# First attention of a fused attention and two-MoE kernel: memory products in two banks, one reciprocal per sequence, loads per sequence, and a new written order

## The chip, the cores and the metric

One core of a Trainium2 chip runs the kernel. The metric is the time of one execution on the device in microseconds (us), as the median over runs. The engines are named as the profile names them: PE is TensorE (matmuls), PEld its weight loads, DVE is VectorE, ACT is ScalarE, POOL is GpSimd and SP is SyncE, which issues all the DMA transfers.

## The reference, cut to what matters

Four sequences of 576 tokens with 8 heads of 64 go through an attention that adds a memory readout, and then through two gated layers with 512 to 1536 to 512 columns. All inputs are f32.

```python
scores = scale * (q @ k.T);  scores[causal] = -1e9          # per batch b, head h
a = exp(scores - scores.max(-1));  a /= a.sum(-1) + 1e-9
local = a @ v
q_p = where(q > 0, q, exp(q) - 1) + 1                       # phi
mem_out = (q_p @ M_prev) / ((q_p @ z_prev) + 1e-6)
g = sigmoid(beta)                                           # per head
x = g * mem_out + (1 - g) * local                           # -> tokens x 512
x = x / sqrt(mean(x * x) + 1e-6) * rms_g
x = (silu(x @ w_gate) * (x @ w_val)) @ w_out                # first MoE layer
x = (sigmoid(x @ w_gate2) * (x @ w_val2)) @ w_out2          # second MoE layer
```

## The kernel before, in words

The tokens go through the layers in five groups. Group -1 holds the first 128 tokens of each of the four sequences (512 tokens); groups 0 to 3 hold the other 448 tokens of one sequence each. While the layers of group g run on TensorE, the attention of group g + 1 is issued in between. A layer works in 12 slices of 128 hidden columns. For each slice `hidden` makes two products, `pg` (gate) and `pv` (value), VectorE and ScalarE make the gated product `t` from them, and `out_share` adds its product with the slice's output weights to the four accumulators `po`. The weights arrive as 64-bit floats (`raw`, `rawl`), ScalarE and VectorE take each block to f32 (`f64_top`, `f64_word`), and split it into a high and a low part.

The change is in what stands ahead of all that: the first attention, that of group -1, which nothing can hide (`att_first`). Its stages are small functions, made for each sequence b and often for each half j of the heads (j = 0 even, j = 1 odd heads), and the string `ORDER` names them in the order in which they are written. A stage's instructions are tied to the one before it on the same engine, so `ORDER` is the order of each engine's queue up to its last name:

- `S` scores of a sequence into two banks, `M` maxima, `X` exponentials, `T` transposes, `C` copies of the transposed weights, `A` products with v;
- `E`, `Em`, `Ph` the feature function phi (ScalarE, GpSimd, VectorE), `P` memory products, `R` and `V` the divisions of memory and local part, `Y` their sum on GpSimd;
- `Q`, `N`, `W`, `F` square, mean, power and norm, `U` transposes of the normed tokens, `H` and `L` their high and low part;
- `wt`, `wo`, `wh`, `wl` the four weight blocks (gate and value) of slices 0 and 1: top, word, high, low;
- `g0a`, `v0a`, `a0a`, `dd0a` (and `g1a` ...) gate, value, tanh and gated product of slices 0 and 1 for the first 256 tokens, the two first sequences;
- `fillN` N matmuls whose result nobody reads, and `G`, `G1` the gates from beta.

Behind `ORDER`, a scheduler places what `hidden`, `weights` and `token_scale` issue, as far as `issue_after` leaves it open. It starts with the second 256 tokens of slices 0 and 1, whose products `pg` and `pv` go into the two banks of the pool `mm`. `out_share` of slice 0 follows, and then slice 2. Weight loads go through four buffers `raw` and two `rawl`; the tile `warm`, which the fillers read, lies in one of the four. `token_scale` takes the largest entry of the norm's weights `g_bc` (`gm`) and scales them for the later groups. SP issues DMAs in the order of its queue, and a `kept` transfer that waits for a word holds those behind it.

Of the kernel before, what the change touches and what calls it, by code (L numbers as in the profile page):

```python
# [9 lines left out]
F32 = mybir.dt.float32  # L10
# [50 lines left out]
def attn_moe_moe_kernel(ctx, tc, qT, kT, qk0, v, mz, beta, w8, rms_g, outT):  # L61
# [6 lines left out]
    nc = tc.nc  # L68
# [36 lines left out]
    ones = const.tile([128, 1], F32, name="ones")  # L105
# [3 lines left out]
    bt = const.tile([128, H], F32, name="bt")  # L109
# [13 lines left out]
    pw = zps.tile([128, 512], F32, tag="fb", name="pw")  # L123
# [94 lines left out]

    def att_load0():
        for b in range(B):  # L220
            z["e", b] = zp.tile([128, NMAX], F32, tag=f"ze{b % 2}", name="e0")
            qk = zp.tile([128, 2, NMAX], F32, tag=f"zqk{b}", name="qk0")
            z["q", b], z["k", b] = qk[:, 0], qk[:, 1]
            nc.sync.dma_start(out=qk, in_=qk0[b])
            if b == 0:
                first_raw.append(load_raw(0, 0, 0))
            if b == 1:
                nc.sync.dma_start(out=bt, in_=beta[None, :].to_broadcast([128, H]))
                z["v"] = zp.tile([128, B, NMAX], F32, tag="zv", name="v0")
                nc.sync.dma_start(out=z["v"], in_=v[:, 0:128, :].rearrange("b s d -> s b d"))  # L230
                load_consts()
            if b == 2:
                first_raw.append(load_raw(0, 0, 1))
        for m in range(2):
            first_raw.append(load_raw(0, 1, m))

    def first_stages(xt):
# [43 lines left out]
        def exps(b, j):  # L281
            z["rs", b, j] = ap_.tile([128, NP], F32, tag="rs", bufs=8, name="rs")
            sc = z["sc", b, j] = zp.tile([128, NMAX], F32, tag=f"zs{j}", bufs=2, name="s0")
            for p in range(NP):
# [7 lines left out]
                    accum_out=z["rs", b, j][:, p:p + 1],  # L292
# [27 lines left out]
        def av_mul(b, j):  # L320
# [1035 lines left out]
```

## Time and profile before

| | before |
|---|---|
| median of 3 runs | 1050.18 us (1047.84 to 1050.64) |
| profiled execution | 1048.04 us |
| span of the profiled execution, first to last instruction | 1046.3 us |
| mean granted TensorE clock | 0.998 of 2.4 GHz |
| PE busy | 1024.9 us (98% of the span) |
| DVE busy | 815.1 us (78%) |
| ACT busy | 590.6 us (56%) |
| POOL busy | 90.8 us (9%) |

The profiled execution lasts 1.7 us longer than its span. Busy shares are means over the whole span; the first 60 us look different from the rest, and have to be read by themselves.

### The profile page before, as it was taken

The page shows a single profiled execution, that of the slowest core. Times are in us where ns is not written, and L with a number is a line of the kernel's source. Part 1 is how long each engine was busy: PE and PEld are TensorE (multiplying, and loading weights), DVE is VectorE, ACT ScalarE, POOL GpSimd, SP SyncE. Part 2 cuts the span into 40 slices and gives each one's busy share as a digit, 9 for nine tenths or more (in the row PEclk, how much of TensorE's full clock was granted, in tenths as well). Part 3 has the DMA queues.
Part 4 walks back from the last instruction along what each step waited for, and adds up shares of the span by engine and source line. Part 5 has one row for each costly group of instructions (what it writes and reads, how often), then busy time and mean ns, then how long its engine had stood idle before and what let it go on. Part 6 is the DMA issues. An engine that isn't in the chain of part 4 may idle for free.

```text
span 1046.3 us, 18459 instructions
## 1 busy us (share of the span) xinstructions
PE 1024.9 (98%) x6801; PEld 774.2 (74%) x6801; DVE 815.1 (78%) x1751; ACT 590.6 (56%) x1118; POOL 90.8 (9%) x85
## 2 busy tenths in 40 slices
PE   8899999999999999999999999999999999999998
PEld 5768887888766777776667867666677777987896
DVE  5969999988759989874677866648788768995882
ACT  5758877776768868862454543425545444542442
POOL 3301001000002102110010101000101000000000
PEclk9999999999999999999999999999999999999999
DMA  7499998984898457678554553585556257846630
GB/s 272 161 360 364 317 389 258 312 275 168 239 348 276 147 213 240 246 249 279 199 168 163 173 187 130 152 281 168 167 174 211 90 175 231 309 146 221 238 121 36
DMA packets 92281, 231.63 MB, mean 221 GB/s; under 512 B 24096, under 2 KB 30240, under 8 KB 92064
## 3 DMA queue, kind: packets, MB, share of 16 engines
q1 hardware_dynamic: 92192, 230.47, 65.2%
q8 instruction: 53, 0.87, 0.3%
q14 instruction: 36, 0.29, 0.1%
HBM read 182.72 MB, written 44.04 MB: 217 GB/s over the span
## 4 chain that ended last, share of the span: by engine, by line
PE 78%; DVE 9%; issue 5%; DMA 4%; ACT 3%; SPq 0%; POOL 0%; ACTq 0%; DVEq 0%; POOLq 0%
PE po L863 23%; PE pg L807 20%; PE pv L807 19%; PE pw L973 6%; PE ps L210 4%; PE pm L580 1%; PE pav L531 1%; PE pav L533 1%; PE pav L532 1%; DMA g_bc<-in_rms_g 1%; DMA ha<-x 1%; PE po L860 1%; DMA raw<-in_w 1%; DMA half<-ws 0%; DVE x L624 0%
## 5 line engine op out<-in xcount | busy, mean ns | idle before, releaser
L863 PE MATMUL po<-h,ws 128*128 128x448 f32 (+1 forms) x468 | 114.3, 385 | 0.2 <-DMA ws<-parts 0.2
L863 PE MATMUL po<-h,wl 128*128 128x448 f32 (+1 forms) x408 | 99.6, 385 | 0.0
L863 PEld LDWEIGHTS po<-h,ws 128*128 128x128 f32 x468 | 86.0, 188 | 11.9 <-ACT h L846 0.4
L515 POOL PARTITION_ALL_REDUCE mb<-mx x32 | 57.0, 1783 | 406.6 <-DVE mx L511 394.7
L827 ACT ACTIVATE t<-pg,unit 128x448 f32<-128x448 f32 x70 | 44.2, 631 | 73.7 <-PE pg L807 73.7
L863 PE MATMUL po<-h,wr 128*128 128x448 f32 x360 | 85.6, 379 | 0.0
L863 PEld LDWEIGHTS po<-h,wl 128*128 128x128 f32 x408 | 75.5, 188 | 9.7 <-ACT h L842 0.2
L807 PEld LDWEIGHTS <-ws 128*128 128x128 f16 x504 | 46.8, 98 | 46.8 <-issue 6.2
L807 PEld LDWEIGHTS <-wr 128*128 128x128 f16 x504 | 46.8, 98 | 44.3 <-issue 4.4
L475 ACT COPY sc<-ps 128x448 f32<-128x448 f32 (+5 forms) x128 | 51.9, 421 | 41.7 <-DVE sc L470 20.8
L842 ACT CAST h<-t 128x448 fp32r<-128x448 f32 (+1 forms) x70 | 40.6, 580 | 55.4 <-DVE t L831 50.5
L863 PEld LDWEIGHTS po<-h,wr 128*128 128x128 f32 x360 | 66.7, 188 | 6.1
L201 ACT ACTIVATE sc<-sc 128x1536 f32<-128x1536 f32 x32 | 47.5, 1485 | 38.1 <-DVE sc L524 26.6
L204 DVE TENSOR_TENSOR pt<-sc,pt 128x1536 f16<-128x1536 f32 x32 | 56.1, 1754 | 10.0 <-ACT pt L203 9.7
L807 PEld LDWEIGHTS <-wl 128*128 128x128 f16 x384 | 35.9, 98 | 33.9 <-issue 4.2
L210 PE MATMUL ps<-qq,kk 128*128 128x448 f32 (+2 forms) x160 | 57.9, 365 | 1.0 <-ACT sc L475 1.0
L843 DVE TENSOR_TENSOR h<-t,h 128x448 fp32r<-128x448 f32 (+1 forms) x70 | 46.2, 659 | 10.8 <-ACT h L842 10.5
L829 DVE SCALAR_TENSOR_TENSOR t<-t,pg 128x448 f32<-128x448 f32 (+2 forms) x50 | 31.0, 620 | 26.3 <-ACT t L827 26.3
L210 PE MATMUL ps<-q,kk 128*128 128x448 f32 (+2 forms) x160 | 49.4, 318 | 0.0
L837 DVE SCALAR_TENSOR_TENSOR t<-t,pv 128x448 f32<-128x448 f32 (+1 forms) x52 | 32.9, 632 | 20.5 <-PE pv L807 19.1
L203 ACT CAST pt<-sc 128x1536 f16<-128x1536 f32 x32 | 47.0, 1468 | 0.3
L807 PEld LDWEIGHTS <-wrl 128*128 128x128 f16 x288 | 26.6, 98 | 26.5 <-issue 3.8
(330 smaller groups left out, 2672.2 us busy)
## 6 DMA issues: line engine op xcount, KB each, us to landing
raw<-in_w SPq DMA_DIRECT2D x50, 511.8 KB, 6.5
ws<-parts SPq DMA_DIRECT2D x32, 512.0 KB, 4.1
wr<-parts SPq DMA_DIRECT2D x32, 512.0 KB, 3.9
wl<-parts SPq DMA_DIRECT2D x26, 512.0 KB, 3.7
kept<-w SPq DMA_DIRECT2D x48, 256.0 KB, 5.3
rawl<-in_w SPq DMA_DIRECT2D x22, 511.8 KB, 7.0
ws<-half SPq DMA_DIRECT2D x21, 512.0 KB, 3.7
wr<-half SPq DMA_DIRECT2D x19, 512.0 KB, 4.1
```

Source lines behind the costliest of these rows:

```text
L201: nc.scalar.activation(out=sc[:, 0:n], in_=sc[:, 0:n], func=AF.Exp, scale=scale)
L203: nc.scalar.copy(out=pt[:, 0, 0:n], in_=sc[:, 0:n])
L204: nc.vector.tensor_tensor(out=pt[:, 1, 0:n], in0=sc[:, 0:n], in1=pt[:, 0, 0:n], op=ALU.subtract)
L210: nc.tensor.matmul(ps[:, c0:c0 + n], kk[:, k0:k0 + 128], r[:, q0:q0 + n], start=(i == 0), stop=(i == 1 and not mask))
L475: nc.scalar.copy(out=sc[:, d:d + n], in_=ps[:, c:c + n])
L515: nc.gpsimd.partition_all_reduce(mb[:, 0:448], mx[:, 0:448], channels=128, reduce_op=bass_isa.ReduceOp.max)
L807: nc.tensor.matmul(ps[:, 0:n], w[:, a, k * 128:(k + 1) * 128], x[b][:, k, o:o + n], start=(i == 0), stop=(i == 3 * KD - 1))
L827: nc.scalar.activation(out=t, in_=pg[:, 0:n], func=AF.Tanh, scale=u[:, 0:1] if half else 0.5)
L842: nc.scalar.copy(out=hi, in_=t)
L843: nc.vector.tensor_tensor(out=lo, in0=t, in1=hi.bitcast(F32), op=ALU.subtract)
L863: nc.tensor.matmul(po[d][:, 0:n], w[2][:, a, c], hh[:, b, 0:n], start=(first and i == 0), stop=(last and i == 2))
L973: nc.tensor.matmul(regions[m][at], left(i, m, a, k), right(j, b, k), start=first and c == 0, stop=c == 5, skip_group_check=True,)
```

## The change

The stages of the first attention are rewritten and reordered.

- Memory products: one stage `P` per sequence fills two banks with the products of all 8 heads, in place of two stages with one bank each.
- Division: `D` makes all 16 divisors of a sequence with one reciprocal (8 for the local part, 8 for the memory part), and `Vm` and `Va` do one 512-wide multiply each. Before there were four groups of combination, reciprocal and 256-wide multiply. Both halves' products with v now go into one bank.
- Loads: `v` and the memory matrices come per sequence, in an order of their own (`LOADS`); beta comes as one row and is spread over the partitions by a one-row matmul (`G0`).
- The copies of the transposed weights all go to ScalarE; before, two of them went to VectorE.
- There are 18 fillers in place of 36, and they read the identity in place of `warm`.
- Slice 1's second 256 tokens get two banks of the pool `ps`. `token_scale` stands behind the last stage of `ORDER`, `dd1a`. The weights of slices 2 to 4 are written behind the gated product of slice 1.

```diff
 ORDER = """
-E0 S0 Em0 wt0 Ma0 Mb0 S1 fill3 Xa0 wo0 Ph0 fill1 Xb0 Ta0 fill1 Ma1 Mb1 Ca0 Tb0 fill1 Xa1 Aa0 fill1
...
+S0 S1 fill4 G0 E0 Ma0 wt0 E1 Em0 Xa0 fill2 Ta0 Mb0 Em1 G1 Ph0 Xb0 P0 Ca0 wo0 E2 fill2 Tb0 Cb0 Ma1
+Mb1 G Xa1 Aa0 fill1 Ab0 wt1 S2 D0 Vm0 Va0 Xb1 Em2 Ph1 wo1 Ta1 Mb2 Y0 Q0 N0 P1 Tb1 Ca1 D1 E3 Xb2
...
-COPY = "DDAA"
...
+    banks = [zps.tile([128, 512], F32, tag=f"pp{i}{j}", name="pw") for i in (0, 2, 1) for j in range(2)]
+    pw = banks[3]
...
+    LOADS = "q0 q1 w0 v0 m0 b q2 v1 m1 g w1 v2 m2 q3 v3 m3 w2 w3"
...
+        def gates_sum():
+            z["bt"] = zps.tile([128, H], F32, tag="pm", name="pb")
+            nc.tensor.matmul(z["bt"], ones, bt, start=True, stop=True)
...
         def fill(n):
             for i in range(n):
-                nc.tensor.matmul(pw, warm[:, 0:128], warm, start=True, stop=True)
+                nc.tensor.matmul(
+                    z.get("unread", pw).rearrange("p (a k) -> p a k", a=4),
+                    ident_b,
+                    ident_b[:, None, :].to_broadcast([128, 4, 128]),
+                    start=True,
+                    stop=True,
+                )
...
-            if j == 0 or COPY[b] == "A":
-                nc.scalar.copy(out=pt, in_=z["ps", b][j])
-            else:
-                nc.vector.tensor_copy(pt, z["ps", b][j])
+            nc.scalar.copy(out=pt, in_=z["ps", b][j])
+            if j:
+                z["unread"] = z["ps", b][1]
...
+        def divisors(b):
+
+            r = z["r", b] = ap_.tile([128, 2, H], F32, tag="r1", bufs=2, name="r1")
+            sums = z["pm"][:, :, 0:260].rearrange("p i (h d) -> p i h d", d=65)[:, :, :, 64]
             nc.vector.scalar_tensor_tensor(
...
+                out=r[:, 0], in0=z["rs", b], scalar=1e-9, in1=igate1, op0=ALU.add, op1=ALU.mult
+            )
...
             nc.vector.reciprocal(out=r, in_=r)
+
+        def mem_mul(b):
             nc.vector.tensor_tensor(
...
+                out=x[:, b, :].rearrange("p (i h d) -> p i h d", i=2, d=64),
+                in0=z["pm"][:, :, 0:260].rearrange("p i (h d) -> p i h d", d=65)[:, :, :, 0:64],
+                in1=z["r", b][:, 1].rearrange("p (i h) -> p i h", i=2)[:, :, :, None].to_broadcast([128, 2, 4, 64]),
                 op=ALU.mult,
             )
...
             for f in range(early):
-                hidden(ws[f], l, f, 256, g, xt, hs[f], 256)
+                hidden(ws[f], l, f, 256, g, xt, hs[f], 256, (("mm", "mm"), ("ps", "pa"))[f])
+                halfway.append(tuple(last_of(e) for e in (mybir.EngineType.Activation, mybir.EngineType.DVE)))
...
-                        with behind(turn):
+                        with behind(turn + (halfway[-1:] if early and f < early + 3 else [])):
                             ws.append(weights(g, l, f))
...
             if l == 0 and g < 0:
-                token_scale()
+                with tc.issue_after(z["gm"]):
+                    token_scale()
```

VectorE, around the first division. Before, its queue holds these rows between the maxima of sequence 1 (`m` from `ps_192`) and the first local division of sequence 0:

```order
L278 TENSOR_REDUCE m_231<-ps_192 128x4
L674 TENSOR_REDUCE gm<-g_bc 128x1
L279 TENSOR_SCALAR m_231<-m_231 128x4
L306 COPY qk_131<-ps_172 128x512
L657 TENSOR_SCALAR pw<-gm 128x1
L659 TENSOR_SCALAR inv<-pw 128x1
L246 TENSOR_SCALAR igate<-igate 128x8
L246 TENSOR_SCALAR igate_100<-igate_100 128x8
L663 RECIPROCAL s_2226<-inv 128x1
L676 TENSOR_SCALAR half_isx<-inv 128x1
L325 SCALAR_TENSOR_TENSOR r_263<-rs,igate_100 128x4
L333 RECIPROCAL r_263<-r_263 128x4
```

With the change the same place, from the same maxima (`ps_197`) on, holds the whole division of sequence 0:

```order
L291 TENSOR_REDUCE m_265<-ps_197 128x4
L292 TENSOR_SCALAR m_265<-m_265 128x4
L249 TENSOR_SCALAR igate<-igate 128x8
L249 TENSOR_SCALAR igate_100<-igate_100 128x8
L337 SCALAR_TENSOR_TENSOR r_298<-rs,igate_100 128x8
L340 SCALAR_TENSOR_TENSOR r_298<-pm,igate 128x8
L348 RECIPROCAL r_298<-r_298 128x16
L351 TENSOR_TENSOR x<-pm,r_298 128x512
L360 TENSOR_TENSOR av<-ps_184,r_298 128x512
```

The `gm` chain (`gm`, `pw`, `inv`, `s`, `half_isx`) and the copy from `ps_172` have left this place, and one reciprocal serves both divisions.

VectorE, at the end of the first attention. Before, from the low part of sequence 2's tokens (`xb` from `ps0_305`) on (numbers tell buffers apart), with the output weights' words (`wo`) and slice 2's first words between the gated products `t`:

```order
L400 TENSOR_TENSOR xb_156<-ps0_305,xa_155 128x4x128
L386 SCALAR_TENSOR_TENSOR qk0_149<-x_159,ri_161,g_bc_101 128x512
L456 SCALAR_TENSOR_TENSOR t_157<-t_157,pg_560 128x256
L677 TENSOR_SCALAR g_bc_101<-g_bc_101,s2_2226 128x512
L457 TENSOR_TENSOR t_157<-t_157,pv_577 128x256
L737 SCALAR_TENSOR_TENSOR wo_650<-raw_651,top0_126 128x512
L737 SCALAR_TENSOR_TENSOR wo_657<-raw_658,top1_128 128x512
L400 TENSOR_TENSOR xb_156<-ps0_415,xa_155 128x4x128
L737 SCALAR_TENSOR_TENSOR w_730<-raw_731,top0_126 128x512
L456 SCALAR_TENSOR_TENSOR t_158<-t_158,pg_600 128x256
L737 SCALAR_TENSOR_TENSOR w_740<-raw_741,top1_128 128x512
L457 TENSOR_TENSOR t_158<-t_158,pv_615 128x256
```

With the change, from the last gated product of the first 256 tokens on:

```order
L486 TENSOR_TENSOR t_172<-t_172,gv_532 128x256
L703 TENSOR_REDUCE gm_2169<-g_bc_101 128x1
L686 TENSOR_SCALAR pw_2171<-gm_2169 128x1
L688 TENSOR_SCALAR inv_2173<-pw_2171 128x1
L692 RECIPROCAL s2_2175<-inv_2173 128x1
L705 TENSOR_SCALAR half_isx_126<-inv_2173 128x1
L706 TENSOR_SCALAR g_bc_101<-g_bc_101,s2_2175 128x512
L858 SCALAR_TENSOR_TENSOR t_171<-t_171,pg_613 128x256
L864 TENSOR_TENSOR t_171<-t_171,pv_626 128x256
L858 SCALAR_TENSOR_TENSOR t_172<-t_172,pg_642 128x256
L864 TENSOR_TENSOR t_172<-t_172,pv_655 128x256
L766 SCALAR_TENSOR_TENSOR w_679<-raw_680,top0_131 128x512
```

All four gated products of the second 256 tokens (`L858`, `L864`) now stand ahead of the first word of slice 2 (`w`), and the `gm` chain stands ahead of them.

SP, where the loads of slices 0 to 3 follow the four first ones. Before (`kept` writes a finished word back, `raw` and `rawl` load a block):

```order
L751 DMA kept_0_0_213<-w_162 128x512
L751 DMA kept_0_0_213<-w_164 128x512
L725 DMA raw_651<-in_w8 128x2047
L751 DMA kept_0_1_430<-w_166 128x512
L725 DMA raw_658<-in_w8 128x2047
L751 DMA kept_0_1_430<-w_168 128x512
L725 DMA raw_731<-in_w8 128x2047
L725 DMA raw_741<-in_w8 128x2047
L725 DMA rawl_750<-in_w8 128x2047
```

With the change:

```order
L780 DMA kept_0_0_252<-w_176 128x512
L754 DMA raw_600<-in_w8 128x2047
L780 DMA kept_0_0_252<-w_178 128x512
L754 DMA raw_607<-in_w8 128x2047
L780 DMA kept_0_1_478<-w_180 128x512
L754 DMA raw_680<-in_w8 128x2047
L780 DMA kept_0_1_478<-w_182 128x512
L754 DMA raw_690<-in_w8 128x2047
L754 DMA rawl_699<-in_w8 128x2047
L754 DMA rawl_761<-in_w8 128x2047
```

Slice 2's first two blocks are the last two `raw` in both. Now each of them stands behind a `kept` of slice 1 (`kept_0_1`), so behind that block's word; the two `rawl` follow as before.

## Rows read from the trace of the kernel before

**Rows 1.** The chain that ended last: start us, us, what.
```profile
20.72 0.44 PE ps L298 x4
...
60.58 3.43 PE po L860 x8
```

**Rows 2.** Waits by engine and line: us in total, times, longest us.
```profile
DVE gm L674 <- DMA g_bc<-in_rms_g: 3.1, 1, 3.1
...
PE ps L312 <- DVE pw L657: 2.9, 1, 2.9
...
PE pg L807 <- DVE t L829: 1.7, 1, 1.7
...
SPq L725 <- PE pw L272: 3.9, 1, 3.9
```

**Rows 3.** Windows: stretch, its length, busy us by engine, PEclk, DMA share, GB/s.
```profile
15.00:20.00 5.00, 3.58 (x18) 3.23 (x19) 4.00 (x19) 2.02 (x9) 0.67 (x1) 0.71 1.03 413
...
60.00:80.00 20.00, 20.00 (x77) 13.94 (x77) 11.53 (x20) 9.93 (x16) 0.00 (x0) 1.00 1.03 370
80.00:160.00 80.00, 80.00 (x467) 65.26 (x466) 78.68 (x148) 64.92 (x107) 7.77 (x4) 1.00 1.00 352
```

**Rows 4.** Timeline of VectorE: start us, us, line, operation, out<-in.
```profile
8.41 0.68 DVE L278 TENSOR_REDUCE m<-ps 128x4 f32<-128x512 f32 x1
...
9.22 0.69 DVE L737 SCALAR_TENSOR_TENSOR w<-raw,top 128x512 int32<-128x512 int32 x1
9.83 0.69 DVE L354 SCALAR_TENSOR_TENSOR e<-qk,e 128x512 f32<-128x512 f32 x1
...
28.75 0.15 DVE L558 SCALAR_TENSOR_TENSOR r<-pm,igate 128x4 f32<-128x4 f32 x1
28.94 0.18 DVE L561 RECIPROCAL r<-r 128x4 f32<-128x4 f32 x1
29.16 0.42 DVE L562 TENSOR_TENSOR x<-pm,r 128x256 f32<-128x256 f32 x1
29.50 0.68 DVE L439 TENSOR_TENSOR ws<-w,ws 128x512 fp32r<-128x512 f32 x1
...
52.90 0.42 DVE L457 TENSOR_TENSOR t<-t,pv 128x256 f32<-128x256 f32 x1
```

**Rows 5.** Timeline, GpSimd's add and power, and the VectorE step beside the add.
```profile
22.99 1.64 POOL L343 TENSOR_TENSOR x<-x,av 128x512 f32<-128x512 f32 x1 [7.33 <-DVE x L562]
23.42 1.76 DVE L737 SCALAR_TENSOR_TENSOR w<-raw,top 128x512 int32<-128x512 int32 x1
...
26.92 0.60 POOL L383 TENSOR_TENSOR ri<-ss,half_neg 128x1 f32<-128x1 f32 x1 [0.40 <-DVE r L558]
```

**Rows 6.** Timeline of ScalarE: first and ninth step of eight exponentials, a square.
```profile
8.61 0.37 ACT L286 ACTIVATE s<-ps,m 128x128 f32<-128x128 f32 x1 [2.24 <-DVE m L279]
...
11.36 0.62 ACT L304 COPY qk<-ps 128x512 f32<-128x512 f32 x1
...
25.75 0.61 ACT L376 ACTIVATE qk<-x 128x512 f32<-128x512 f32 x1
```

**Rows 7.** Timeline of TensorE: scores, filler, products with v, half passes.
```profile
22.09 0.59 PE L261 MATMUL ps<-ident_b,tri_b 128*128 128x512 bf16 x2
...
23.71 0.39 PE L272 MATMUL pw<-warm 128*128 128x512 bf16 x1
23.94 1.00 PE L312 MATMUL ps<-v,qk 128*128 128x64 f32 x8
24.77 0.38 PE L272 MATMUL pw<-warm 128*128 128x512 bf16 x1
...
52.01 0.28 PE L807 MATMUL pg<-xa,ws 128*128 128x256 f32 x1
...
53.45 0.28 PE L807 MATMUL pv<-xa,ws 128*128 128x256 f32 x1
```

**Rows 8.** DMA issues: out<-in, engine, count, KB each, median us from issue to landing.
```profile
v<-in_v SPq DMA_DIRECT2D x1, 1024.0 KB, 8.9
```

More of the change, by code (lines that the diff above doesn't have):

```diff
@@ L104, in attn_moe_moe_kernel @@
     nc.vector.tensor_copy(tri4_b, tri4)
-    ones = const.tile([128, 1], F32, name="ones")
+    ones = const.tile([1, 128], F32, name="ones")
     nc.vector.memset(ones, 1.0)
@@ L217, in attn_moe_moe_kernel, with load @@
     z = {}
+    LOADS = "q0 q1 w0 v0 m0 b q2 v1 m1 g w1 v2 m2 q3 v3 m3 w2 w3"
     def att_load0():
+        def load(kind, i):
+            if kind == "q":
+                qk = zp.tile([128, 2, NMAX], F32, tag=f"zqk{i}", name="qk0")
+                z["q", i], z["k", i] = qk[:, 0], qk[:, 1]
+                nc.sync.dma_start(out=qk, in_=qk0[i])
+            elif kind == "v":
+                z["v", i] = zp.tile([128, NMAX], F32, tag=f"zv{i}", name="v0")
+                nc.sync.dma_start(out=z["v", i], in_=v[i, 0:128, :])
+            elif kind == "m":
+                nc.sync.dma_start(
+                    out=mzt[:, i].rearrange("p a j e -> p (a j e)"), in_=mz[:, i * NP * 130:(i + 1) * NP * 130]
+                )
+            else:
+                first_raw.append(load_raw(0, i // 2, i % 2))
         for b in range(B):
             z["e", b] = zp.tile([128, NMAX], F32, tag=f"ze{b % 2}", name="e0")
[L222 to L235, printed above, removed]
+        for name in LOADS.split():
+            if name == "b":
+                nc.sync.dma_start(out=bt, in_=beta[None, :])
+            elif name == "g":
+                nc.sync.dma_start(out=g_bc, in_=rms_g[None, :].to_broadcast([128, DM]))
+            else:
+                load(name[0], int(name[1:]))
     def first_stages(xt):
@@ L281, in exps @@
         def exps(b, j):
-            z["rs", b, j] = ap_.tile([128, NP], F32, tag="rs", bufs=8, name="rs")
+            if ("rs", b) not in z:
+                z["rs", b] = ap_.tile([128, H], F32, tag="rs", bufs=4, name="rs")
             sc = z["sc", b, j] = zp.tile([128, NMAX], F32, tag=f"zs{j}", bufs=2, name="s0")
@@ L341, in av_add @@
         def av_add(b):
-            xs = x[:, b, :].rearrange("p (a j d) -> p j a d", j=2, d=64)
-            nc.gpsimd.tensor_tensor(out=xs, in0=xs, in1=z["av", b], op=ALU.add)
+            nc.gpsimd.tensor_tensor(out=x[:, b, :], in0=x[:, b, :], in1=z["av", b], op=ALU.add)
         def phi_exp(b):
@@ L354, in phi, with mem @@
             nc.vector.scalar_tensor_tensor(out=e, in0=z["q", b], scalar=0.0, in1=e, op0=ALU.max, op1=ALU.add)
-        def mem(b, i):
-            z["pm"] = zps.tile([128, 2, 2, 65], F32, tag="mm", name="pm")
-            for j in range(2):
-                t = 2 * i + j
+        def mem(b):
+            z["pm"] = zps.tile([128, 2, 512], F32, tag="pm", name="pm")
+            for t in range(NP):
                 nc.tensor.matmul(
-                    z["pm"][:, j].rearrange("p a b -> p (a b)"),
+                    z["pm"][:, t // 2, 130 * (t % 2):130 * (t % 2) + 130],
                     z["e", b][:, 128 * t:128 * t + 128],
@@ L411, in first_stages @@
                 for name, f in dict(
-                    M=maxima, X=exps, T=transposes, C=copies, A=av, V=av_mul, P=mem, R=mem_mul
+                    M=maxima, X=exps, T=transposes, C=copies, A=av
                 ).items():
@@ L1135, in att_first @@
                 z["hi"] = before[mybir.EngineType.Activation]
-            if name == "Vb3":
+            if name == "dd1a":
+                z["gm"] = before[mybir.EngineType.DVE]
+            if name == "Va3":
                 z["lo"] = before[mybir.EngineType.DVE]
```

89 lines of the change are left out of this document (47 added, 42 removed).

## The prediction

> **What bounds the kernel now.** I read the chain of waits first, then the windows, the waits by engine, and the timelines of the first 64 us. From 60.6 us on the chain is TensorE work almost without a break: it starts with the output share of slice 0 [rows 1]. Whatever stands ahead of that instruction is paid in full, and nothing after it depends on a clock time of its own. So the question is when that `po` starts (60.6 us on the chain), and whether what comes behind it can follow an earlier start.
>
> Ahead of it VectorE sets the pace, and two of its stops are not work. It waits 3.1 us for `g_bc` to land, at `gm`, which stands in its queue between the two maxima of sequence 1. TensorE stops 1.7 us at the second-half `pg` of slice 1, for the bank that slice 0's gated product still holds [rows 2]. A third stop is SP's: the load of slice 2's second weight block waits 3.9 us on the filler matmuls, because `warm` shares its buffer with that load [rows 2].
>
> Behind it, from 80 to 160 us, VectorE is busy 78.7 of 80 us while TensorE is busy all the time: both are full. From 60 to 80 us VectorE is busy only 11.5 of 20 us [rows 3]. That is a reserve of 8.5 us.
>
> **The change, part by part.** Steps are charged start to start.
>
> VectorE: a maximum with its scaling 0.8 (8.41 to 9.22), a 512-wide step 0.6 (9.22 to 9.83), a small combination 0.2, a reciprocal 0.2, a 256-wide multiply 0.34 (28.75 to 29.50) [rows 4]; a norm, 512 wide with a third operand, is charged 0.7. Each sequence had four groups of combination, reciprocal and multiply, 0.75 each, so 3.0 us. It now has two combinations, one reciprocal of 16 numbers and two 512-wide multiplies out of PSUM: 0.2 + 0.2 + 0.25 + 0.6 + 0.6 = 1.85. No row shows a 16-wide reciprocal; it lies between the 4-wide one (0.2) and a 256-wide step (0.34), and I take 0.25. Saved: 1.15 a sequence, 4.6 in all. The two 512-wide copies that VectorE gives up save 1.2 more and cost ScalarE two copies, 0.62 each with the overlap to the next step, 0.5 as I charge them start to start [rows 6]. The `gm` chain leaves this place (0.6 + four small ones, 1.4, and the 3.1 us wait) and comes back behind the last gated product, where it delays only `L858`, whose reader `po` comes 3 us later.
>
> GpSimd: the same eight 512-wide steps. One of them cost a VectorE step 1.76 us in place of 0.68 [rows 5]. Over four adds that is between 0 and 4.3 us; rows of before have it now and then, so I take 1.4 on the path.
>
> Rather than add savings that overlap, I walk the new order with these steps. ScalarE: eight exponentials 2.75 us (8.61 to 11.36), so 1.4 for four; a square 0.6, and a weight's top counted like a square [rows 6]. TensorE: scores 1.62 (22.09 to 23.71), four products with v 0.83 (23.94 to 24.77), four transposes 0.44, a half pass over a weight block 1.44 (52.01 to 53.45) [rows 1, 7]. GpSimd: an add 1.64, a power 0.6 [rows 5].
>
> - Sequence 0: its second maximum starts at 8.4 as now [rows 4]; nothing ahead of it changes. Exponentials 8.6 to 10.0; the gate exponentials wait for the one-row product behind the fillers, to 10.55; second four to 11.9. Copy 12.4, the feature exponential of sequence 2 to 13.0, second copy 13.5. Products with v end at 14.9, `Va0` at 15.6.
> - Sequence 1: ScalarE goes on at 13.5: four, a top, four, to 17.1. The add of sequence 0 runs 15.6 to 17.2, its square to 17.9, its norm ends at 19.3. Copy 18.4, a feature exponential 18.9, four exponentials of sequence 2 to 20.3, copy 20.8. Products end 22.35, `Va1` 23.0.
> - Sequence 3: its scores need the banks of sequence 0, read last by `L0` at 22.2, and stand behind two fillers: 22.8 to 24.4. Maxima to 26.05. ScalarE is full: exponentials 26.0 to 28.8, copies to 30.5. Products end 31.7, `Va3` 32.35.
> - Its tail: add 34.0, square 34.6, mean 34.75, power 35.4, norm 36.1, transposes 37.0, `H3` 37.55. `L3` ends at 39.1, since two `wo` words and `L2` stand ahead of it.
> - Second halves: `pg` of slice 0 starts at 39.1 (now 52.0, [rows 7]): 12.9 us. Its four half passes now have four banks of their own: 39.1 + 5.8 = 44.9 against 60.6 for `po` [rows 1].
>
> So the walk gives 60.6 - 44.9 = 15.7 us. Off it go 1.4 for GpSimd, and 1.1 for margins that have become thin: the low part of slice 2's first block comes out of VectorE at about 47.0, and `pg` of slice 2 is due at 44.9 + 3.0 = 47.9, by 0.9 us only. 15.7 - 2.5 = 13.2. The profiled execution took 1048.04 us with a span of 1046.3 (2.2 under the median of 1050.18, inside the three runs' 1047.84 to 1050.64): 1048.0 - 13.2 = 1034.8, said as **1035 us**.
>
> What hides the edits that I cost at nothing: half of the fillers (18 of 36) go, and were behind waits of others; the one-row product for the gates is one small matmul behind four fillers, and costs up to 0.5 if `bt` lands late. The loads: `q2` is now the seventh load, behind 2.6 MB; before, 2.6 MB had landed when the 1 MB `v` did, 8.9 us after its issue at 2.6, so at 11.5 [rows 8]. It is needed at 12.4. If that cover is gone, each microsecond stands on the path, since the second copy of sequence 0 is queued behind that feature exponential on ScalarE, and products, scores and all of sequence 1 behind the copy. The Trainium skill (DMA: Bandwidth & Descriptors, Rules for kernel authors) says the opposite of this edit: 128 partitions and 1 MiB or more in one transfer, small ones put together; here `v` and the memory matrices go from one transfer of 1 MB to four of a quarter. My estimate from that page's table (341 GB/s at 1 MB, 138 at 64 KB) is that `q2` comes 1 to 2 us later, which makes 1036 of 1035. No row of before shows such a quarter load beside others, and the sum keeps to the row: 0.
>
> SP: slice 2's blocks are now issued at about 31, 34 (its words), and 36 twice (the two `rawl` buffers lie over sequence 2's `qk` tile, so they wait for its transposes). They are used from 44 us on. Even 9 us to land would be in time, so loads give no term.
>
> **The rivals.**
> 1. *VectorE takes part back.* `po` comes 15.7 us earlier, but VectorE's own last gated product of the first 256 tokens ends at 40.5 with `gm` to 41.9 behind it, against 53.3 [rows 4]: 11.4 us earlier. For it: the full stretch 80 to 160. Against it: the 8.5 us of reserve in 60 to 80, which cover the 4.3 us of difference. If they do not, 1048.0 - 11.4 + 1.4 = 1038; if weights of slices 2 to 4 are late as well, by 2 to 4 us, 1040 to 1042.
> 2. *The clock falls (slower).* TensorE stood idle for 2.9 us ahead of a product with v that waited for VectorE's `gm` chain [rows 2], and from 15 to 20 us it was granted 0.71, so partly the level of 1.2 GHz [rows 3]. With 18 fillers fewer, the same may happen between 9 and 48 us. The work there is 30 us at 2.4 GHz: scores 3.2, twelve groups of transposes 5.3, products with v 6.6, memory products 3.6 (counted like products with v), eight half passes 11.5. At 1.2 GHz it takes up to twice that, and `po` would start at 9.1 + 60 = 69, so 1057. The walk leaves TensorE idle for 5.8 of its 35.8 us, so the sign turns from about 21 us of work at the lower level on (15.7 + 5.8). Taken at 24 to 30 us of it, 1050 to 1057. Against it: in my walk no gap on TensorE is above 1 us. The Trainium skill (TensorE: Matmul & The Clock Gate, Why this matters for your kernels) warns of this: idle gaps between bursts bring the clock back to its half level. The trace agrees for that one gap of 2.9 us.
> 3. *It is a wash.* The `gm` wait and the bank wait are the only gains, and a new stall of 2 to 3 us (`bt`, `q2`, a bank order I misread) eats them: 3.1 + 2.1 - 2.5 = 2.7, so 1045 to 1048.
>
> **How the numbers follow.** Forecast (13 us, with 11 to 17): 0.68. Rival 1: 0.17. Rival 3: 0.08, of which half is within 0.3%. Rival 2: 0.05. Lower still than 1031: 0.02. The range runs from the full walk with no deduction and a little more (1030) to where rival 3 begins (1044). Its lower end takes in GpSimd at nothing, its upper end GpSimd at 4.3 and rival 1. A change of 0.3%, about 3 us, is what a measurement of this kernel can tell from none: faster 0.90, same 0.05, slower 0.05.
>
> **What would show it.** Right: no VectorE wait on `g_bc`; the first second-half `pg` at 38 to 41 us, no TensorE wait on slice 0's gated product, `po` at 44 to 48; the granted clock at 1.00 in 10 to 45; gap to before still 12 to 16 us at 160. Wrong: `po` early but TensorE waiting on `ws` or `wl` low parts between 45 and 80 (rival 1), a granted clock near 0.5 over several windows (rival 2), or ScalarE waiting for `qk` or the gates (rival 3).

## The result and the profile after

The changed kernel takes 1035.94 us (median of 4 runs, 1035.2 to 1037.05); the kernel before takes 1049.46 us on the same chip (4 runs, 1047.84 to 1050.64). The ratio is 0.9873, with a 95% interval of 0.9856 to 0.989. The profiled execution took 1035.77 us with a span of 1034.0, against 1048.04 and 1046.3 before.

The chain that ended last, after: start us, us, what.

```profile
47.57 6.87 PE po L889 x16
54.43 2.80 PE pg L836 x12
...
60.03 2.76 PE pg L836 x12
...
160.33 3.04 PE pg L836 x12
```

The last two of these gate products, those of slice 3 and of the next layer's start, in the chain of before:

```profile
72.96 2.73 PE pg L807 x12
...
173.77 3.02 PE pg L807 x12
```

`po` starts at 47.57 in place of 60.58 [rows 1]: 13.0 us earlier. One thing is new: `po` of slices 0 and 1 run as one block of 16 matmuls, and slice 2's gate product stands behind both. At slice 3's gate product, where both kernels have done the same work again, the gap is 72.96 - 60.03 = 12.9, at 160 us it is 173.77 - 160.33 = 13.4, and at the end of the span 1046.3 - 1034.0 = 12.3. So the time was won ahead of `po`, and little was lost behind it. (In a timeline a matmul starts some tenths of a us before its piece of the chain, since its record overlaps the one before it: `po` at 47.41 for 47.57. The starts of `po` and of slice 6 below are read from timelines, those at 160 us from the chain.)

Windows after: stretch, its length, busy us by engine (PE, PEld, DVE, ACT, POOL), PEclk, DMA share, GB/s.

```profile
10.00:15.00 5.00, 5.00 (x41) 4.47 (x41) 3.35 (x11) 4.44 (x21) 1.49 (x1) 1.00 1.02 341
15.00:20.00 5.00, 5.00 (x48) 4.12 (x47) 4.41 (x10) 4.60 (x19) 2.49 (x3) 1.00 1.03 404
...
60.00:80.00 20.00, 20.00 (x94) 16.36 (x93) 17.39 (x34) 13.03 (x23) 0.39 (x1) 1.00 1.04 368
80.00:160.00 80.00, 78.71 (x472) 63.48 (x471) 78.01 (x146) 64.03 (x109) 9.57 (x4) 1.00 0.93 338
```

The first 13 us behind `po`, after:

```profile
47.00:60.00 13.00, 13.00 (x46) 8.08 (x45) 11.62 (x20) 11.02 (x19) 0.00 (x0) 1.00 0.88 314
```

The same two stretches behind `po` in the kernel before:

```profile
60.00:73.00 13.00, 13.00 (x46) 8.15 (x46) 8.35 (x15) 7.52 (x12) 0.00 (x0) 1.00 1.05 375
...
73.00:93.00 20.00, 20.00 (x94) 16.37 (x93) 16.15 (x32) 13.32 (x24) 0.70 (x1) 1.00 1.02 367
```

The granted clock from 15 to 20 us is 1.00 in place of 0.71, and TensorE is never without work there. VectorE is busy 17.39 of 20 us from 60 to 80, in place of 11.53 [rows 3], but everything has moved by 13 us, so that this window holds later work than before. Over the same 33 us behind `po`, VectorE is busy 11.62 + 17.39 = 29.0 us in place of 8.35 + 16.15 = 24.5. So 4.5 of the 8.5 us that it had free there are used. From 80 to 160 TensorE has 1.3 us without work that it did not have before.

Waits after, in the first 62 us: us in total, times, longest.

```profile
ACT top L760 <- DMA raw<-in_w: 2.5, 2, 2.1
...
DVE av L360 <- PE ps L325: 1.7, 1, 1.7
...
PE pg L836 <- DVE xb L420: 0.8, 1, 0.8
```

VectorE's 3.1 us wait on `g_bc` and TensorE's 1.7 us wait for the bank [rows 2] are gone. TensorE's longest stop from 9 us to `po` is now the 0.8 us for `xb`, the low part of sequence 3's tokens.

Timeline of VectorE after: start us, us, line, operation, out<-in, [idle before <-releaser].

```profile
12.33 0.17 DVE L337 SCALAR_TENSOR_TENSOR r<-rs,igate 128x8 f32<-128x8 f32 x1
12.42 0.16 DVE L340 SCALAR_TENSOR_TENSOR r<-pm,igate 128x8 f32<-128x8 f32 x1
12.61 0.25 DVE L348 RECIPROCAL r<-r 128x16 f32<-128x16 f32 x1
12.90 0.69 DVE L351 TENSOR_TENSOR x<-pm,r 128x512 f32<-128x512 f32 x1
...
16.45 1.76 DVE L766 SCALAR_TENSOR_TENSOR w<-raw,top 128x512 int32<-128x512 int32 x1
...
23.53 2.37 DVE L379 SCALAR_TENSOR_TENSOR e<-qk,e 128x512 f32<-128x512 f32 x2
...
31.60 0.82 DVE L766 SCALAR_TENSOR_TENSOR w<-raw,top 128x512 int32<-128x512 int32 x1
...
34.35 1.73 DVE L459 TENSOR_TENSOR ws<-w,ws 128x512 fp32r<-128x512 f32 x1
...
40.32 1.29 DVE L420 TENSOR_TENSOR xb<-ps,xa 128x512 fp32r<-128x512 f32 x2
```

GpSimd's four adds after; beside each stands one of the four steps from 16.45 to 34.35 above:

```profile
16.02 1.64 POOL L368 TENSOR_TENSOR x<-x,av 128x512 f32<-128x512 f32 x1 [1.32 <-DVE av L360]
...
23.70 1.65 POOL L368 TENSOR_TENSOR x<-x,av 128x512 f32<-128x512 f32 x1 [2.47 <-DVE av L360]
...
30.60 1.27 POOL L368 TENSOR_TENSOR x<-x,av 128x512 f32<-128x512 f32 x1 [1.99 <-DVE r L337]
...
33.85 1.68 POOL L368 TENSOR_TENSOR x<-x,av 128x512 f32<-128x512 f32 x1 [1.97 <-DVE av L360]
```

The division costs what the prediction took (0.25 us for the reciprocal of 16). Three VectorE steps beside an add take 1.76, 2.37 for two, and 1.73 us, in place of 0.68 each. Each of them ends 0.55 us behind the add (16.02 + 1.64 = 17.66 against 18.21; 25.35 against 25.90; 35.53 against 36.08). So does the step beside the fourth add (31.87 against 32.42), which starts late and so takes only 0.82. Before, one step beside each of the four adds takes longer than its kind too: the first in [rows 5], the others here. The small one ends with its add (35.36 and 35.33), the others 0.55 us behind it:

```profile
34.84 0.52 DVE L279 TENSOR_SCALAR m<-m 128x4 f32<-128x4 f32 x1
...
39.19 1.25 DVE L439 TENSOR_TENSOR ws<-w,ws 128x512 fp32r<-128x512 f32 x1
...
45.37 1.17 DVE L439 TENSOR_TENSOR ws<-w,ws 128x512 fp32r<-128x512 f32 x1
```

### The profile page after: what moved, and what is told of

It is laid out like the page before. It is cut to its first block, busy times and chain, and to the rows that moved or that the text cites. A ratio compares the mean times of both kernels' runs of the same rounds, so it can differ in the third digit from the quotient of the medians.

```text
span 1034.0 us, 18403 instructions
## 1 busy us (share of the span) xinstructions
PE 1018.8 (99%) x6785; PEld 770.8 (75%) x6785; DVE 811.3 (78%) x1721; ACT 589.4 (57%) x1120; POOL 89.6 (9%) x85
## 4 chain that ended last, share of the span: by engine, by line
PE 82%; DVE 8%; issue 4%; ACT 4%; DMA 2%; POOL 0%; SPq 0%; ACTq 0%; DVEq 0%; POOLq 0%
PE po L892 24%; PE pg L836 20%; PE pv L836 20%; PE pw L1002 6%; PE ps L203 4%; PE pm L609 2%; PE pav L560 1%; PE pav L562 1%; PE pav L561 1%; DMA ha<-x 1%; PE po L889 1%; DMA out_T<-o 1%; DVE x L653 1%; DVE xn L648 1%; DMA kept<-w 1%
## 5 line engine op out<-in xcount | busy, mean ns | idle before, releaser
L858 DVE SCALAR_TENSOR_TENSOR t<-t,pg 128x448 f32<-128x448 f32 (+2 forms) x50 | 31.0, 620 | 24.9 <-ACT t L856 24.9
L866 DVE SCALAR_TENSOR_TENSOR t<-t,pv 128x448 f32<-128x448 f32 (+1 forms) x52 | 32.9, 633 | 18.8 <-PE pv L836 17.8
L560 PE MATMUL pav<-vh,pt 128*128 128x65 f16 x448 | 45.4, 195 | 0.5 <-ACT pt L196 0.5
```

The costliest lines, as they stand in the source:

```text
L560: nc.tensor.matmul(ps, ph, vh1[:, vt, h, :], start=first, stop=False)
```

## The experiments

Each run has a ratio to the kernel before, with an interval of about 1.4 to 2.5 us to each side. Smaller differences are read from the trace, at `po` and at 160 us: between 290 and 470 us the profiled executions drift apart by up to 2.3 us, also for kernels that agree within 0.1 us at 268 us, so the end of the span doesn't tell them apart. Part of the drift is the clock: from 370 to 390 us it was granted at 1.00 in the execution of the change, and at 0.91 in those of `a_gm_free`, `a_no_fill`, `a_no_tie` and `a_old_order`. Slices are counted in the chain; the gate product that starts at 86.7 us after is that of slice 6, and the expectations below call it slice 5's.

**What each part gave.** Six edits, in seven runs, undo or take over one part each.

The `gm` tie, put into the kernel before (`b_gm_late`) and taken out of the changed one (`a_gm_free`):

```diff
+            if name == "dd1a":
+                z["gm"] = before[mybir.EngineType.DVE]
...
             if l == 0 and g < 0:
-                token_scale()
+                with tc.issue_after(z["gm"]):
+                    token_scale()
```

> The kernel before with one edit: the gm chain (largest entry of g_bc and its scaling) stands behind the last gated product of the first 256 tokens, as the change has it. Theory (po is set by VectorE's queue, and each of the change's parts gives its own few us): the 3.1 us wait and 1.4 us of chain leave the path, so 3 to 5 us faster than before, near 1045, with no VectorE wait on g_bc and the half clock of 15 to 20 us gone or smaller. Rival (gm alone makes most of the gain): 9 us or more faster. Rival (the gain is elsewhere, the wait was hidden): within 1.5 us of before.

> The changed kernel without the tie that puts gm behind dd1a; the scheduler then places gm between the two maxima of sequence 1 again. Theory: g_bc was issued at 5.5 us and took 7.9, so VectorE stands until 13.4 in place of going on at 11.1; most of that 2.3 us plus 1.4 of chain hides in the 1.7 us that Va0 waits for its products, so 1 to 2.5 us slower than the change, 1037 to 1038.5. Rival (the wait is the main part of the gain): 4 us or more slower. Rival (ScalarE sets the pace there, VectorE has room): within 0.7 us.

In the kernel before: 1046.1 us, ratio 0.9967 (0.9953 to 0.9982), so 3.5 us faster, as the theory said. `po` starts at 55.18, and the granted clock from 15 to 20 us is 1.00 in place of 0.71, though nothing else was changed there:

```profile
15.00:20.00 5.00, 4.84 (x44) 3.97 (x44) 4.42 (x11) 2.57 (x6) 1.70 (x2) 1.00 1.03 408
```

So `po` gains 5.2 us, and part of it comes back: slice 6's gate product starts at 97.20 (before 100.53, so 3.3 us are left), behind scores that waited for ScalarE.

```profile
96.83 0.36 PE L210 MATMUL ps<-qq,kk 128*128 128x192 f32 x1 [0.71 <-ACT sc L475]
```

Taken out of the changed kernel, `gm` goes back between the maxima; VectorE stands 1.3 us for `g_bc`, and `po` starts at 48.75, 1.3 us later (1.3 at 160 us too), as the theory said. Ratio 0.9886 (0.9873 to 0.9899).

The second pair of banks (`a_one_bank`):

```diff
-                hidden(..., 256, (("mm", "mm"), ("ps", "pa"))[f])
+                hidden(..., 256, ("mm", "mm"))
```

> The changed kernel with slice 1's second 256 tokens in the same two banks of mm as slice 0's, as before. Theory: pg of slice 1 waits for slice 0's gated product, which ends at 45.8 while TensorE comes to it at about 44.5; so po starts 1 to 2 us later and the kernel takes 1037 to 1038. Rival (something else holds po, since the gated product has to be there for po anyway): within 0.6 us of the change.

```profile
44.85 0.38 PE L836 MATMUL pg<-xa,ws 128*128 128x256 f32 x1 [0.65 <-DVE t L858]
```

The wait for slice 0's gated product is back, at 0.65 us, and `po` starts at 47.82: 0.4 us later (0.6 at 160 us). That is the rival's size and not the theory's: the bank is a small term. Ratio 0.9881 (0.9868 to 0.9894).

The division (`a_div_groups`): four combinations, four reciprocals and four 256-wide multiplies a sequence, in the same stages.

```diff
-            nc.vector.reciprocal(out=r, in_=r)
+            for i in range(2):
+                c = slice(4 * i, 4 * i + 4)
...
+                nc.vector.reciprocal(out=r[:, 0, c], in_=r[:, 0, c])
...
+                nc.vector.reciprocal(out=r[:, 1, c], in_=r[:, 1, c])
```

> The changed kernel with the division of each sequence in four groups again: four combinations, four reciprocals, four 256-wide multiplies, in the same places of the written order. Theory: 1.15 us more of VectorE a sequence; sequence 0's hides in the 1.7 us that VectorE waits for products with v, the others lie on the path, so po starts 1.5 to 3.5 us later than 47.4 and the kernel takes 1.5 to 3.5 us more than the change, with no wait behind po to give any of it back. Rival (VectorE has room there, ScalarE or the products with v set the pace): po within 0.7 us of 47.4.

`po` starts at 48.77, 1.36 us later, and the gap is still 1.4 at 160 us; ratio 0.9884 (0.9864 to 0.9904). This is just below the theory's low end. The small steps of four groups take 1.07 us (12.03 to 13.10) in place of 0.57 (12.33 to 12.90); two 256-wide multiplies take 0.67 up to the next step (14.74 to 15.41), one 512-wide 0.61 (15.24 to 15.85). So against this edit a sequence saves 0.50 + 2 x 0.06 = 0.6 us. The edit is not the division of before, though: there each group's multiply stands right behind its own reciprocal, and the group takes 0.75 us [rows 4], 3.0 a sequence; here the four small groups stand together, and the sequence takes 1.07 + 2 x 0.67 = 2.4. What the layout of before would cost in the new order was not run.

The loads (`a_loads_whole`): `v` and the memory matrices in one transfer each, in the order of before.

```diff
-    LOADS = "q0 q1 w0 v0 m0 b q2 v1 m1 g w1 v2 m2 q3 v3 m3 w2 w3"
+    LOADS = "q0 w0 q1 b V M g q2 w1 q3 w2 w3"
```

> The changed kernel with v and the memory matrices as one load each again and the loads in the order of before. Theory (bytes ahead of a load decide, not the size of a piece): q of sequence 2 then stands behind about 4.3 MB and lands at 13 us or later, where ScalarE wants it at 12.5, so po is 0.5 to 2 us later and the kernel up to 2 us slower. The Trainium skill (DMA: Bandwidth & Descriptors, Rules for kernel authors) prefers transfers of 1 MiB and more; by that rule the loads come 1 to 2 us earlier and the kernel is not slower. Rival (loads have slack either way): within 0.5 us.

```profile
15.33 0.63 ACT L378 ACTIVATE e<-qk 128x512 f32<-128x512 f32 x1 [2.79 <-DMA qk<-in_qk]
```

ScalarE waits 2.79 us for `q` of sequence 2 and the copy behind it is as late; `po` starts at 49.99, 2.6 us later. The ratio is 0.9888 (0.9872 to 0.9904). In the changed kernel the same step at 12.46 us waits for nothing, with quarter loads at 341 to 404 GB/s (windows above). The edit changes the size of the loads and their order at once. The whole loads move about as fast, 367 and 412 GB/s in the same windows (below), so that what is left for the 2.6 us is the order, by which more bytes stand ahead of `q2`.

```profile
10.00:15.00 5.00, 3.75 (x29) 3.11 (x28) 3.56 (x12) 2.31 (x13) 0.00 (x0) 1.00 1.01 367
15.00:20.00 5.00, 3.98 (x40) 3.28 (x39) 2.20 (x3) 4.52 (x19) 2.91 (x2) 1.00 1.02 412
```

The written order (`a_old_order`): each new stage where the stages that it replaces stood, and 36 fillers.

```diff
 ORDER = """
-S0 S1 fill4 G0 E0 Ma0 wt0 E1 Em0 Xa0 fill2 Ta0 Mb0 Em1 G1 Ph0 Xb0 P0 Ca0 wo0 E2 fill2 Tb0 Cb0 Ma1
+E0 S0 Em0 wt0 Ma0 Mb0 S1 G0 fill3 Xa0 wo0 Ph0 fill1 Xb0 Ta0 fill1 Ma1 Mb1 Ca0 Tb0 fill1 Xa1 Aa0
...
```

> The changed kernel with the stages written in the order of before (and its 36 fillers): each new stage stands where the old ones that it replaces stood (one division, one memory product, one local multiply a sequence), all else of the change stays. Theory (po's start follows the walk along the written order, and undoing the parts one by one gave only 1.3 for gm, 0.4 for the bank, 1.4 for the division and 2.6 for the loads of the 13.0 us): the order makes 4 to 8 us, so po starts at 51 to 55.5 and the kernel takes 1040 to 1044. Rival (the new stages make the gain, the order little): po within 2 us of 47.4.

`po` starts at 54.57, 7.2 us later, and the kernel takes 1043.47 us, ratio 0.9939 (0.9924 to 0.9955). Both lie in the theory's range, and of the edits made this one costs the most. It is not the order alone: 18 more fillers come with it, and a lower clock. TensorE waits up to 1.9 us at once for a norm there, with 20 to 25 us its least busy window, and in the next the granted clock is 0.66:

```profile
20.00:25.00 5.00, 3.27 (x26) 2.59 (x24) 4.44 (x8) 3.31 (x13) 3.97 (x3) 1.00 0.89 309
25.00:30.00 5.00, 4.70 (x20) 2.85 (x20) 4.72 (x10) 4.73 (x14) 2.22 (x2) 0.66 0.15 59
```

The tie of the weights of slices 2 to 4 to slice 1's gated product (`a_no_tie`):

```diff
-                        with behind(turn + (halfway[-1:] if early and f < early + 3 else [])):
+                        with behind(turn):
```

> The changed kernel without the tie that writes the weights of slices 2 to 4 behind slice 1's gated product; the scheduler may put their words and low parts between the gated products again. Theory (po of slice 0 needs the gated product alone, and slice 2's weights are not needed before 53.9): words ahead of the gated products hold po by 0.6 to 2.5 us, and the kernel is 0 to 2.5 us slower. Rival (slice 2's weights are the ones that are short of time, so writing them earlier helps): po the same and the time 0.5 us or more faster.

1040.21 us, ratio 0.9908 (0.9892 to 0.9924): 0.35% or 3.7 us more than the change, and `po` of slice 0 starts at 53.27, 5.9 us later. That is the theory's direction and more than its size. At 160 us about 3 of the 5.9 us are left, since part of slice 2's gate product now runs ahead of slice 0's `po`. VectorE after this edit:

```profile
45.28 0.69 DVE L766 SCALAR_TENSOR_TENSOR w<-rawl,top 128x512 int32<-128x512 int32 x1 [1.31 <-ACT top L760]
...
49.06 0.69 DVE L766 SCALAR_TENSOR_TENSOR w<-raw,top 128x512 int32<-128x512 int32 x1 [0.30 <-ACT top L760]
...
50.33 0.69 DVE L766 SCALAR_TENSOR_TENSOR w<-raw,top 128x512 int32<-128x512 int32 x1 [0.52 <-ACT top L760]
...
51.07 0.41 DVE L858 SCALAR_TENSOR_TENSOR t<-t,pg 128x256 f32<-128x256 f32 x1
```

Words of slices 2 and 3 stand ahead of the gated product, and each waits for a top on ScalarE that waits for its load. TensorE stands 3.49 us for the bank that this `t` frees.

**The clock, and what a still earlier `po` is worth.** Five runs start `po` earlier than the change does.

No fillers (`a_no_fill`):

```diff
-            for i in range(n):
+            for i in range(0):
```

> The changed kernel with none of the 18 fillers inside ORDER (the 9 ahead of it stay); their results are read by nobody. Theory (fillers lie in waits and cost nothing, and the granted clock of 1.00 does not hang on them): within 1 us of the change, clock 1.00 in every 5 us stretch of 10 to 45. Rival (the fillers hold the clock; the clock rival of the prediction): granted clock between 0.5 and 0.8 in several stretches, and 3 us or more slower. A third way: TensorE's queue is freed of work that stood ahead of something needed, and it is 1 us or more faster.

The granted clock is 1.00 in every 5 us stretch up to 50 us, also where TensorE has the most room:

```profile
15.00:20.00 5.00, 4.28 (x40) 3.60 (x36) 4.19 (x10) 4.85 (x20) 3.25 (x3) 1.00 1.03 408
...
25.00:30.00 5.00, 4.18 (x38) 4.06 (x36) 4.83 (x15) 4.03 (x19) 0.94 (x2) 1.00 0.02 9
```

Its longest stop on TensorE in 9 to 48 us is 0.9 us. `po` starts at 46.42, 1.0 us earlier, and at 160 us nothing is left of it (160.35 against 160.33). About half is lost at slice 3's gate product, which waits 0.22 us for VectorE at 59.26, and the rest at that of slice 6, which starts at 86.62, behind a wait. Ratio 0.9883 (0.9866 to 0.99).

```profile
86.62 0.50 PE L836 MATMUL pg<-xa,ws 128*128 128x512 f32 x1 [0.25 <-DVE t L858]
```

The adds on VectorE (`a_add_dve`), each right behind `Va`:

```diff
-            nc.gpsimd.tensor_tensor(out=x[:, b, :], in0=x[:, b, :], in1=z["av", b], op=ALU.add)
+            nc.vector.tensor_tensor(out=x[:, b, :], in0=x[:, b, :], in1=z["av", b], op=ALU.add)
```

> The changed kernel with the four adds of memory and local part on VectorE, each right behind its local multiply, in place of GpSimd. VectorE gets four steps of 0.6 us; the steps that ran 0.4 to 1.1 us long beside an add go back to 0.68, and sequence 3's tail is an add of 0.7 in place of 1.6. Theory (contention with GpSimd is the term that the prediction charged too low): po starts 1 to 2.5 us before 47.4. Second part of the theory (the run without fillers had po 1.0 us earlier and lost it at the gate product of slice 5, which waited for VectorE): the time stays within 0.7 us of the change. Rival (all that stands ahead of po is paid in full, as the prediction said): the time falls by as much as po. Rival (GpSimd costs VectorE nothing): po 1 us later or more.

```profile
16.36 0.68 DVE L766 SCALAR_TENSOR_TENSOR w<-raw,top 128x512 int32<-128x512 int32 x1
...
23.32 1.28 DVE L379 SCALAR_TENSOR_TENSOR e<-qk,e 128x512 f32<-128x512 f32 x2
...
34.22 0.68 DVE L459 TENSOR_TENSOR ws<-w,ws 128x512 fp32r<-128x512 f32 x1
```

The long steps are back at 0.68, 1.28 for two and 0.68: 1.08 + 1.09 + 1.05 = 3.2 us less. The four added steps cost 2.4 (an estimate, four of 0.6), and `po` starts at 46.21, 1.2 us earlier. Again it is gone by slice 6, 0.4 us of it at slice 3:

```profile
86.57 0.50 PE L836 MATMUL pg<-xa,ws 128*128 128x512 f32 x1 [0.48 <-DVE t L858]
```

1035.97 us, ratio 0.9855 (0.9837 to 0.9873); the interval overlaps that of the change, and at 160 us the two kernels agree within 0.03 us.

The output weights' words behind `L3` (`a_wo_late`):

```diff
-            if name == "Va3":
+            if name == "L3":
                 z["lo"] = before[mybir.EngineType.DVE]
```

> The changed kernel with the two words of the output weights of slices 0 and 1 behind the last low part (L3), so 1.2 us of VectorE leave the place ahead of the second halves. Theory: the second-half pg starts 0.7 to 1.2 us earlier and po too, but the gate product of slice 5 stays at 86.6 us, where it waits for VectorE, and the time is within 0.5 us of the change. Rival (paid in full): 1 us faster.

`po` starts at 47.15, 0.3 us earlier; in this execution ScalarE stood 2.2 us for loads of `q` ahead of it in place of 1.1, so the edit's own size can't be read. The gate product of slice 6 starts at 88.56, not at 86.6; VectorE, which it waits for, had stood 2.5 us for a k load and 0.8 us for a `kept` transfer. 1036.27 us, ratio 0.9862 (0.9847 to 0.9878): no gain shown.

Two runs then try to lift what holds slice 6. `a_add_wait2` starts group 0's attention one output share later, `a_add_qk_first` puts its first k and q loads ahead of its v load; both have the adds on VectorE.

```diff
-        wait = 2 if g == 0 else 1
+        wait = 2 if g <= 0 else 1
```

```diff
+        if g == 0:
+            yield lambda: att_qk(g, 0)
         yield lambda: att_v(g)
...
-                yield lambda h=h: att_qk(g, h)
+                if g or h:
+                    yield lambda h=h: att_qk(g, h)
```

> The changed kernel with the adds on VectorE (po 1.2 us earlier) and, besides, the attention of group 0 begun one output share later, so that its loads and first VectorE steps leave the stretch of 60 to 86 us, where VectorE stood 2.75 us for a load of kd. Theory (the gate product of slice 5 is held by this work of VectorE): it starts at 85.4 to 85.7 in place of 86.6, TensorE has no gap there, and the time falls by up to 1.2 us below the change unless the work that was moved is missing a cover later. Rival (VectorE and TensorE are both full from 80 to 160, so what is moved comes back as a gap behind 90 us): the time within 0.5 us of the change or up to 3 us slower, with PE below 79 of 80 us in 80 to 160.

> The changed kernel with the adds on VectorE (po 1.2 us earlier, lost again at the gate product of slice 5) and, besides, the first k and q loads of group 0's attention issued ahead of its 1.25 MB of v, in place of behind it. Theory (that gate product is held by VectorE, which stood 2.75 us at 63.4 for the k load behind the v load): no wait of VectorE above 1 us on kd, the gate product of slice 5 at 85.3 to 86.0 in place of 86.6, no gap ahead of it, and the time up to 1.2 us below the change. Rival (VectorE stands for v next, or the rest of the way to 160 us has no room): the gate product of slice 5 at 86.4 or later, or gaps behind it, and the time within 1 us of the change or slower.

The first starts slice 6's gate product at 85.78, but takes 1042.33 us, ratio 0.9932 (0.9916 to 0.9949). The attention of group 0 is now late at the end of the group, and the product that needs its tokens waits 8.0 us:

```profile
PE pg L836 <- DMA ha<-x: 8.0, 1, 8.0
```

The rival had the side right; its size is twice what I gave it, and it lies at 270 us and not between 90 and 160, so its mechanism is not what happened: it is the cover missing later that the theory had set as its own condition. The second has VectorE's `kk` at 63.38 in place of 66.11 with no wait, and yet slice 6's gate product starts at 87.12 (`po` at 46.89), with waits of 0.71 us at 60.23 and 0.50 at 91.41. 1037.46 us, ratio 0.988 (0.9855 to 0.9904). The rival holds: the k load by itself was not what set it. No version here is shown to beat the change.

One thing that no run takes apart is the rate of the loads. From 56 to 87 us the DMA share is 1.00 to 1.05, so the DMA engines are busy throughout, in the changed kernel and in those with an earlier `po`, and ScalarE's waits for loads from 47 to 87 us grow as `po` comes earlier. After, and then with the adds on VectorE (`a_add_dve`):

```profile
ACT top L760 <- DMA raw<-in_w: 2.9, 2, 2.4
ACT kk L185 <- DMA kd<-in_kT: 1.5, 1, 1.5
```

```profile
ACT top L760 <- DMA raw<-in_w: 3.5, 3, 1.8
ACT kk L185 <- DMA kd<-in_kT: 2.8, 1, 2.8
```

VectorE's `kk` behind that k load starts at 65.64 us after, and at 66.16 (`a_no_fill`) and 66.11 (`a_add_dve`) with `po` 1.0 and 1.2 us earlier. So VectorE stands for a load that does not come earlier with `po`.

## Why the prediction was right, step by step

- **What bounds the kernel.** Right. 13.0 us at `po` are 13.4 at 160 us, and the signs that the prediction named came out: no wait on `g_bc`, the first second-half `pg` at 40.6 us, `po` at 47.4, a granted clock of 1.00. Later starts of `po` are paid in full to 160 us (`a_div_groups` 1.4, `a_loads_whole` 2.6, `a_old_order` 7.2; not `a_no_tie`, where other work runs ahead of `po`). Earlier ones are not, which the sentence "whatever stands ahead of that instruction is paid in full" missed: 1.0 and 1.2 us were lost by slice 6, so the change stands just where this rule ends. In the kernel before it is the same with `gm` alone: 5.2 us at `po`, 3.3 at slice 6.
- **The walk.** Up to `Va0` each step came within 0.3 us: the second copy at 13.28, `Va0` ending at 15.85. From there it ran late by the adds: the second maximum of sequence 3 by 1.4 us, `L3` (41.5 against 39.1) by 2.4, `po` (47.4 against 44.9) by 2.5. The two deductions, 1.4 + 1.1, were as large, so 13.2 met 13.0. That it met it to 0.2 us is luck: the first deduction was too small, and the second was for something that did not happen.
- **GpSimd, taken as 1.4.** Mis-sized. The three long steps cost 3.2 us, and the step beside the fourth add 0.1 more. "Rows of before have it now and then" was read off one row, and the trace of before has it beside all four adds, 2.5 us in all (1.76 [rows 5], 1.25 and 1.17 in place of 0.68, 0.52 in place of 0.17); the bound of 4.3 was nearer. The Trainium skill (SBUF — State Buffer, SBUF: two separate sides) says that VectorE with two inputs from SBUF and GpSimd hold one pair of ports in turn, each for a whole instruction. The trace agrees for the adds: after, each of the four steps ends 0.55 us behind its add. It does not agree for GpSimd's step with a scalar, of which the last section tells. A VectorE multiply out of PSUM beside the add at 30.60 took 0.69.
- **Margins, taken as 1.1.** Wrong place. Slice 2's first low part came at 50.0, later than the 47.0 forecast, but its gate product was not due at 47.9: both `po` stand ahead of it, so it started at 53.87 and waited for nothing. The margins that are gone are at slices 3 and 6.
- **The division, 1.15 a sequence.** The new price is right: 1.85 was taken, and the steps take 0.57 + 0.61 + 0.61 = 1.8. The old one, 3.0, is read rightly from the rows of before. No run shows the difference: `a_div_groups` packs its groups more tightly than before had them (2.4 a sequence), so its 0.6 us by the steps and 1.36 us at `po` measure a smaller step. The forecast does not rest on it, since the walk uses the new price alone.
- **`gm`.** Right: 3.5 us in the kernel before, against 3.1 of wait and 1.4 of chain. In the new order it is worth 1.3: VectorE waits 1.3 us for `g_bc` there, to 12.94, in place of 3.1 to 15.01 before.
- **The loads.** Right by the row: `q2` was in time. Whole transfers in the order of before cost 2.6 us, since `q2` then stands behind them. The rule of the Trainium skill (DMA: Bandwidth & Descriptors, Rules for kernel authors), transfers of 1 MiB and more, gave an estimate of 1 to 2 us the other way; the trace does not bear it out here.
- **Fillers at nothing.** Right for the clock, and more than that: without any, `po` starts 1.0 us earlier. So the 18 that are left are not all behind waits of others.
- **What was not priced.** The tie of the weights of slices 2 to 4. I saw in the order that all gated products stand ahead of slice 2's words, gave it no term, and it is 3.7 us.
- **The rivals.** VectorE takes part back: not at this size (4.5 of 8.5 us of reserve used, 4.3 forecast), but what the runs with an earlier `po` add is lost by slice 6. The clock falls: no; the only fall that the runs of the changed kernel show ahead of `po` is in the old order, behind a stop of 1.9 us. A wash: no. Its 2.1 us for the bank are more than the 1.7 of the rows, and the bank was worth 0.4.

Undoing the parts one by one gives at `po` 7.2 (order, with its fillers), 5.9 (tie), 2.6 (loads), 1.4 (division), 1.3 (`gm`) and 0.4 (bank), 18.8 in all against 13.0, so they overlap. The copies that went to ScalarE and the memory products in two banks were not tried by themselves. What holds slice 6's gate product stays open in part: VectorE's gated product of slice 5 is the last to come, and moving the k load ahead did not help. That the loads as a whole hold VectorE back is the rival that is left.

## What to carry to other kernels

In front of a chain with no gaps, walk the queues along the written order; every microsecond counts, but only up to the point behind it where another engine or the loads have no reserve left (here slices 3 and 6), and that point should be priced beside the gain. When a stage is moved, look at what is written behind it with no tie: work for later that waits for its own loads slips ahead of the work that is due. A load's place in the queue, by bytes ahead of it, mattered more here than the size of the transfers.

## What I had not expected of the hardware

A VectorE step with two inputs from SBUF does not run slower beside a GpSimd add but ends 0.55 us behind it, four times out of four. Beside GpSimd's minimum with a scalar it is otherwise: a norm that starts at 19.78 us, 0.04 behind that step, takes 1.11 in place of 0.75 us and ends at 20.89, ahead of the step's end at 21.23. Another VectorE step with two such inputs (`e`, at 9.19) starts 0.87 us behind the start of that minimum's step for another sequence (8.32, 1.50 us long) and takes 0.69, no longer than alone. Four times the width cost a small VectorE step little: the 16-wide reciprocal took 0.25 us, the 4-wide 0.18.
